# Other homes for x, the output weights and the spatial weights in a delta-rule and gated-MLP kernel on one core

## The chip, the cores and the metric

The kernel runs on one NeuronCore of a Trainium2 chip. The core has five engines with their own instruction streams: TensorE (PE) multiplies matrices from SBUF into PSUM; VectorE (DVE), ScalarE (ACT) and GpSimd (POOL) work on tensors element by element; SyncE (SP) issues all the DMAs here. They wait for each other by semaphores alone. POOL cannot reach PSUM, so whatever comes out of a matmul passes DVE or ACT.

The metric is the device time of one execution in microseconds, as the median of several runs.

## The reference

Attention by the delta rule, whose output is the input of a gated MLP. All is fp32.

```python
# q, k, v: (4, 8, 768, 48); beta: (4, 8, 768)
k_n = k / (norm(k, axis=-1) + 1e-6)
state = zeros((B, H, D, D))
for t in range(S):
    y[:, :, t] = einsum('bhd,bhde->bhe', q[:, :, t], state)
    v_old = einsum('bhde,bhd->bhe', state, k_n[:, :, t])
    state = state + beta_t * einsum('bhd,bhe->bhde', k_n[:, :, t], v[:, :, t] - v_old)
x = y.transpose(0, 2, 1, 3).reshape(4, 768, 384)

h = maximum(x @ w_in, 0.0)                  # w_in: (384, 1024)
u, v = h[..., :512], h[..., 512:]
v_n = (v - mean(v)) / sqrt(var(v) + 1e-6)   # over the last axis
v_s = einsum('ts,bsd->btd', w_spatial, v_n) + b_spatial[None, :, None]
out = (u * v_s) @ w_out                     # w_out: (512, 384)
```

## The kernel before

**The recurrence.** Time is cut into chunks of 64 tokens. Two batches with their 8 heads run side by side, so there are 24 steps: 0 to 11 for batches 0 and 1, 12 to 23 for batches 2 and 3. A step (`step`, with `kqt`) is a chain: `kqt` multiplies K and Q on PE and DVE masks the product (L801); PE multiplies K by the state, DVE subtracts that from v (L827); PE applies the chunk's solved triangle and ACT copies the result (L856); PE multiplies it by K again and DVE adds that to the state (L869, a copy at L871 in steps 0 and 12); PE makes the outputs and ACT copies them (L886).

**The groups.** Four steps make a group, and their triangular systems are solved together in advance by `prep(g)`. Its long part, the lane work, is a column by column sweep of multiplications (L647) and additions (L652). `LANES` gives it to DVE or POOL: for groups 1 and 3 all of it runs on POOL, in the tile set B; for groups 2, 4 and 5 it is shared between DVE and POOL, in the set A; group 0 is solved by blocks of 16. Behind the lane work stand a transpose on DVE and copies and memsets of halves on ACT and POOL; then `widen(g)` finishes the solve with matmuls, and the group's steps may start.

**The MLP.** Two steps make a pair J of 128 tokens in each of two batches. `convert(J)` splits the pair's x into a high and a low fp32r part (tiles xh and xl). Each product is made as high x high, high x low and low x high. `mlp_v` and `mlp_u` multiply x by `w_in` (V matmuls of 128x512, 18 a pair; U matmuls of 128x256, 36 a pair), `norm_v` and `split_v` make v_n of it. `gate(b)` follows for a batch when its six pairs are there: `mlp_g` multiplies v_n by the spatial weights (gate matmuls of 128x256, in three thirds of two halves, 36 each), DVE adds the bias (L1020), u is multiplied in, the result is split again, and `mlp_o` multiplies it by `w_out` (output matmuls of 128x384, 24 a third). A batch has 216 gate and 72 output matmuls.

**What sets the order.** No instruction is placed by hand. `Plan.add` collects operations with what they read and write, a duration, a priority `pr` and the buffers of which they take (`acq`) or free (`rel`) a unit. `Plan.run` then goes through time and gives each engine the ready operation of lowest priority number; the table TUNE adds one number to the priority of each kind of operation in each group's phase. What comes out is emitted engine by engine, and each engine executes its list strictly in order. Where an operation may run on DVE or POOL, the plan chooses. When PE would be idle for long it is given filler, a matmul on the constant tile fl whose result nobody reads.

**Buffers that the change touches.** The pool `x` has one home, (xh, xl), and a second, (la, wl), that is given to it after the last group's solve. So a pair's x is converted when the matmuls of the pair before it are done. The pool `st` has one unit, the tile g0 of 2048 columns. Through it go three loads of spatial weights (256 rows each, L423), each split into wsp_h and wsp_l; then four loads of output weights, each decoded from 64-bit floats by a series of operations on DVE, ACT and POOL (`load_f64`, L475 to L484) and split into wout_h and wout_l. Then g0 is given to the pool `g`, which has no other unit until step 23 is done; `mlp_g` needs one to start. wsp_h, wsp_l, wout_h and wout_l are in use until then: their space holds the solved triangles of groups 0 to 2, the set B, and K for the group products. So `weights2`, called after step 11, first waits for all of that as one condition (the name "early").

K and Q of a step are loaded by `load(s)` with 120 and 126 of the tile's 128 rows, and K for the group products with 121; the rest is zero from the first loads. Each head's 48 rows lie in 64, so rows 112 to 127 are all zero.

Of the kernel before, what the change touches and what calls it, by code (L numbers as in the profile page):

```python
# [1171 lines left out]
```

## Time and profile before

| | us |
|---|---|
| timed runs | 501.27, 489.70, 496.47 |
| median of them | 496.47 |
| the profiled execution, its own time | 490.77 |
| its span, from the first to the last instruction | 489.0 |
| state copies of steps 0 and 12 (L871) start at | 71.2 and 192.2 |

The page that the prediction quotes gives for each engine the time in which it is busy, then digits for forty slices of the span (9 means at least 90% busy; PEclk is the clock granted to TensorE in tenths of full speed). A view by stage gives the same for chosen stretches. A list of groups has one line per kind of instruction, with its count and duration, and a list of waits says who waited for whom. An fp32 matmul of a step, and a filler, counts as two instructions, an fp32r matmul of the MLP as one.

### The profile page before, as it was taken

The numbers are of one execution on the slowest core, as the hardware profiler recorded it, in microseconds if no ns is written. First come the engines' busy times: TensorE is split into PE (matmuls) and PEld (weight loads), VectorE is DVE, ScalarE is ACT, GpSimd is POOL, SyncE is SP. The second block draws the span as 40 slices with busy tenths as digits, with TensorE's granted clock in tenths as the row PEclk, the third lists the DMA queues.
The fourth block names the chain that finished last, engine by engine and source line by source line (L and its number), as shares of the span: only waits on it lengthen the run. The fifth ranks groups of instructions, "written<-read, shape, count | busy, mean of one in ns | idle before, by whom it ended". The sixth has DMA issues, their size and how long they took to land.

```text
span 489.0 us, 20367 instructions
## 1 busy us (share of the span) xinstructions
PE 430.8 (88%) x9094; PEld 382.3 (78%) x9094; DVE 284.0 (58%) x636; ACT 241.8 (49%) x520; POOL 157.7 (32%) x291
## 2 busy tenths in 40 slices
PE   5818688889889998789899799999999999999997
PEld 4605576678668786768678689999998999999996
DVE  4899778987888863436979532632033433452240
ACT  4686662378826387858541341727423394131111
POOL 3149899756897740133562200000000000000000
PEclk9767557998989998999979899999999999999999
DMA  8951134522325653444551002000021000001002
GB/s 268 353 155 43 45 91 111 154 60 82 87 77 143 186 158 122 137 121 132 154 152 40 34 16 95 1 34 0 17 80 35 9 2 33 1 17 50 32 11 87
DMA packets 24882, 41.92 MB, mean 86 GB/s; under 512 B 3608, under 2 KB 13976, under 8 KB 24794
## 3 DMA queue, kind: packets, MB, share of 16 engines
q1 hardware_dynamic: 24794, 40.62, 26.9%
q8 instruction: 71, 1.16, 1.0%
q14 instruction: 17, 0.14, 0.1%
HBM read 34.71 MB, written 4.72 MB: 81 GB/s over the span
## 4 chain that ended last, share of the span: by engine, by line
PE 64%; DVE 11%; ACT 9%; issue 7%; DMA 4%; POOL 3%; SPq 1%; POOLq 0%; ACTq 0%; DVEq 0%
PE ps L542 64%; DMA bn<-in_bun 2%; DMA xs<-xs 2%; ACT wsp_h L406 1%; DVE pt L801 1%; ACT wsp_l L406 1%; DVE prod L647 1%; ACT xt L406 1%; ACT gt L939 1%; DVE ps L652 1%; DMA wout_h<-in_k_t 1%; SPq L423 1%; DVE hd L616 1%; DVE ut L481 1%; POOL hd L647 1%
## 5 line engine op out<-in xcount | busy, mean ns | idle before, releaser
L542 PE MATMUL ps<-wsp_h,vf 128*128 128x256 f32 x480 | 97.0, 287 | 0.0
L542 PEld LDWEIGHTS ps<-wsp_h,vf 128*128 128x128 f32 x480 | 78.5, 191 | 0.7
L542 PE MATMUL ps<-wsp_l,vf 128*128 128x256 f32 x240 | 68.1, 284 | 0.0
L462 POOL TENSOR_TENSOR bn<-bn,nn 128x384 f32<-128x384 f32 x24 | 22.3, 931 | 119.1 <-DMA bn<-in_bun 98.3
L1020 DVE TENSOR_TENSOR gt<-ps,bbc 128x512 f32<-128x512 f32 x24 | 16.6, 691 | 56.3 <-PE ps L542 56.3
L542 PEld LDWEIGHTS ps<-wsp_l,vf 128*128 128x128 f32 x240 | 45.7, 190 | 0.0
L652 POOL TENSOR_TENSOR wsp_l<-wsp_l,wsp_h 128x60 f32<-128x60 f32 (+15 forms) x60 | 37.9, 631 | 2.2
L542 PE MATMUL ps<-wout_h,g 128*128 128x384 f32 x128 | 34.8, 340 | 1.3 <-ACT g L1025 1.2
L647 POOL TENSOR_TENSOR wsp_h<-wsp_l 128x60 f32<-128x60 f32 (+15 forms) x60 | 33.3, 555 | 2.3
L542 PE MATMUL ps<-bn 64*64 64x64 f32 x832 | 21.0, 245 | 12.9 <-DVE pt L801 7.8
L1025 ACT CAST g<-gt 128x512 fp32r<-128x512 f32 x16 | 9.9, 620 | 43.4 <-DVE gt L460 35.4
L542 PEld LDWEIGHTS ps<-bn 64*64 64x64 f32 x832 | 17.4, 154 | 17.7 <-DVE pt L801 8.7
L652 DVE TENSOR_TENSOR ps<-ps,prod 128x192 f32<-128x192 f32 (+13 forms) x90 | 29.5, 327 | 2.2
L647 DVE TENSOR_TENSOR prod<-ps,la 128x192 f32<-128x192 f32 (+13 forms) x90 | 28.7, 319 | 2.0
L856 ACT COPY w<-ps 128x384 f32<-128x384 f32 x24 | 11.5, 478 | 28.7 <-PE ps L542 24.9
L542 PEld LDWEIGHTS ps<-wout_h,g 128*128 128x128 f32 x128 | 23.3, 188 | 2.1 <-ACT g L1025 1.5
L1041 ACT COPY ob<-ps 128x384 f32<-128x384 f32 x24 | 11.5, 479 | 27.1 <-PE ps L542 26.8
L869 DVE TENSOR_TENSOR s<-s,ps 112x384 f32<-112x384 f32 x20 | 11.0, 548 | 22.0 <-PE ps L542 18.7
L542 PE MATMUL ps<-wsp_h,bn 128*128 128x256 f32 x96 | 23.3, 282 | 0.0
L929 ACT ACTIVATE vr<-ps 128x512 f32<-128x512 f32 x22 | 13.1, 596 | 18.5 <-PE ps L542 18.4
L542 PE MATMUL ps<-wout_l,g 128*128 128x384 f32 x64 | 21.9, 342 | 0.0
L1025 ACT CAST xt<-gt 128x512 fp32r<-128x512 f32 x8 | 5.0, 620 | 34.2 <-DVE gt L460 34.2
(227 smaller groups left out, 1158.4 us busy)
## 6 DMA issues: line engine op xcount, KB each, us to landing
bn<-in_bun SPq DMA_DIRECT2D x48, 192.0 KB
bn<-in_bun SPq DMA_DIRECT2D x22, 252.0 KB
bn<-in_bun SPq DMA_DIRECT2D x22, 240.0 KB
out<-ob SPq DMA_DIRECT2D x24, 192.0 KB
vf<-in_w_in SPq DMA_DIRECT2D x6, 512.0 KB
ke<-in_k_t SPq DMA_DIRECT2D x12, 242.0 KB
g<-in_w_sp SPq DMA_DIRECT2D x3, 768.0 KB
g<-in_w_out SPq DMA_DIRECT2D x4, 384.0 KB
```

The lines of the kernel that those rows point to most:

```text
L406: (nc.scalar.copy if e == "ACT" else ENG[e].tensor_copy)(out=out_, in_=in_)
L423: return P.add("SP", dur, lambda: nc.sync.dma_start(out=out_() if callable(out_) else out_, in_=in_() if callable(in_) else in_), rd, wr, ...
L462: nc.gpsimd.tensor_tensor(out=out, in0=in0, in1=in1, op=op)
L542: nc.tensor.matmul(o, l, r, start=start, stop=stop)
L647: P.add(eng, cost(n * m), lambda: ENG[eng].tensor_tensor(out=dst if fst else pt, in0=w[:, :n, j : j + 1].broadcast_to([128, n, m]), in1=la ...
L652: P.add(eng, cost(n * m), lambda: ENG[eng].tensor_tensor(out=dst, in0=dst, in1=pt, op=ALU.add), rd=[pk], wr=[key], pr=p0 + 2)
L856: P.add("ACT", 0.48, lambda: nc.scalar.copy(out=v3(w, 192), in_=v3(pc, 512)[:, :, 0:192]), rd=["pc"], wr=[("w", s % 2)], pr=pr)
L869: P.add("DVE", 0.55, lambda: nc.vector.tensor_tensor(out=sv, in0=sv, in1=pv, op=ALU.add), rd=["pc"], wr=["S"], pr=pr)
L929: P.add("ACT", 0.6, lambda: nc.scalar.activation(out=raw_(r), in_=bank(h.unit), func=AF.Relu, accum_out=st[:, j : j + 1]), rd=[("pv", i)], ...
L1020: P.add("DVE", 0.69, lambda: nc.vector.tensor_tensor(out=gt(), in0=v3(bank(h.unit), 256), in1=bbc[0][:, th * 256 : th * 256 + 256].unsquee ...
L1025: P.add("ACT", 0.6, lambda: nc.scalar.copy(out=gv(gg)[0][:, hs], in_=gt_[t.unit]), rd=[kk], wr=[("gh", b, th, half)], pr=q)
L1041: P.add("ACT", 0.48, lambda: nc.scalar.copy(out=ob_[t.unit], in_=bank(h.unit)[:, :DM]), rd=[("po", b, th, o)], wr=[("ob", b, th, o)], pr=d ...
```

## The change

1. **x.** Pairs 2 and 4 put xh and xl into a second home, the pool `x2`: the first 1536 columns of a new tile wla, which before that holds the triangles of group 0.
2. **Output weights.** They come first. g0 is used as two halves of 768 columns (pool `st` with two units), and each of four loads of 128 rows is decoded in place, with a scratch of 384 columns per half in the tile of kd, tn6 and, later, the bias. The waits are taken apart: every operation waits for what it overwrites and no more.
3. **Spatial weights.** They come second, in six loads of 128 rows through the same two halves. wsp_l is two tiles, wla (2048 columns) and wlb (2560); the triangles of groups 0, 1 and 2 lie in wla, wlb and wsp_h. g0 is given to the gate when they are split.
4. **The bias** is loaded from `weights2`, since its tile is the scratch of the decode.
5. **K and Q** are loaded with 112 rows, after step 1, and K for the group products from step 10 on.
6. TUNE has other numbers, and the plan's time for fetching instructions, FETCH, is 4.1 in place of 3.9.

```diff
-SW, SFREE, FETCH = 30.0, 0.15, 3.9
+SW, SFREE, FETCH = 30.0, 0.15, 4.1
 TUNE = [
-    -11.9, 0, 43.3, 32.1, 0, 0, 0, 0.9, -23.9, 0, -63.7, -115.6, 13.3, -38, 12.6, -55.9, 5, -10.6, -4.4, 0.1,
+    17.4, 14.9, 0, 15.3, -55.5, 43.1, 0, -2.8, -28, 13.8, -16.3, 3.8, 2.9, -11.6, 42.6, 10.5, -1.9, 6.9,
...
-    early = [tagged(t, NT * SEQ) for t in ("wsp_h", "wsp_l")] + [tagged(t, ND * DM) for t in ("wout_h", "wout_l")]
+    early = [tagged(t, n) for t, n in (("wsp_h", NT * SEQ), ("wla", 2048), ("wout_h", ND * DM), ("wout_l", ND * DM), ("wlb", NT * SEQ - 2048))]
...
-        "B": (early[1][:, 2048:3104], early[1][:, 3104:4160], early[0][:, 4096:4352], early[0][:, 4352:4544]),
+        "B": (early[0][:, 2048:3104], early[0][:, 3104:4160], early[0][:, 4160:4416], early[0][:, 4416:4608]),
...
-    xA = lambda h: h.get(lambda u: [tagged(t, NK * 256, F32R) for t in u])
+    def xA(h):
+        def make(u):
+            if u != "x2":
+                return [tagged(t, NK * 256, F32R) for t in u]
+            return [w_("wla")[:, i * NK * 256 : (i + 1) * NK * 256] for i in range(2)]
+        return h.get(make)
+    X2 = (2, 4)
+    xp_ = lambda J: "x2" if J in X2 else "x"
...
-            return early[g // 2][:, g % 2 * 2048 : g % 2 * 2048 + 2048]
+            return early[(1, 4, 0)[g]][:, 0:2048]
...
+    P.pool("x2", ["x2"])
-    P.pool("st", ["g0"])
+    P.pool("st", [0, 1])
...
     def weights2():
-        P.add("X", 0.0, None, wr=[("x", s, q) for s in range(3 * GP) for q in ("d0", "o0", "z1", "d1")] + [("la", "B"), ("w", "B"), ("prod", "B"), ("hd", "B")] + [("ke", i) for i in range(2, 8)] + ["early", "gi", "tn6"])
-        for idx in range(NT // 2):
+        xk = lambda a, b: [("x", k, q) for k in range(a, b) for q in ("d0", "o0", "z1", "d1")]
+        P.add("X", 0.0, None, wr=xk(0, GP) + [("early", 1)])
+        P.add("X", 0.0, None, wr=xk(GP, 2 * GP) + ["gi", ("early", 4)])
+        P.add("X", 0.0, None, wr=xk(2 * GP, 3 * GP) + [("la", "B"), ("w", "B"), ("prod", "B"), ("hd", "B"), ("prod2", "B"), ("early", 0)])
+        P.add("X", 0.0, None, wr=[("ke", i) for i in range(2, 8)] + [("early", 2)])
+        P.add("X", 0.0, None, rd=[("early", 1)], wr=[("xh", J) for J in X2] + [("xl", J) for J in X2] + [("early", 3)])
+        P.add("X", 0.0, None, wr=["kd", "tn6", ("early", "e")])
+        for idx in (2, 3, 4, 5, 0, 1):
...
-            ld(lambda t=t: v3(t()[:, 0:1536], SEQ), w_sp[idx * 256 : idx * 256 + 256].rearrange("(a p) n -> p a n", p=128), wr=[key], pr=due(9) + 5 * idx, acq=[("st", h)], kb=1100)
+            ld(raw, w_sp[idx * 128 : idx * 128 + 128], wr=[key], pr=due(11) + 2 * idx, acq=[("st", h)], kb=393)
+            P.add("ACT", act_t(SEQ), lambda raw=raw, idx=idx: nc.scalar.copy(out=wsp_("wsp_h", 3 * idx, 3), in_=raw()), rd=[key, ("early", 0)], wr=[(key, "h")], pr=due(12) + 0.5 * idx)
+            for i, n in ((6, 2), (8, 1)) if idx == 2 else ((3 * idx, 3),):
+                P.add("", both(256 * n), port=True, bias=BIAS, fn=lambda e, raw=raw, i=i, n=n: tt(e, wsp_("wsp_l", i, n), raw()[:, i % 3 * 256 : (i % 3 + n) * 256], wsp_("wsp_h", i, n), ALU.subtract),
+                      rd=[key, (key, "h"), ("early", 4 if i > 7 else 3 if i < 6 else 1)], wr=[(key, "l", i)], pr=due(12) + 0.5 * idx, rel=[("st", h)])
...
         for idx in range(ND):
-            load_f64(key, w_out[idx * 128 : idx * 128 + 128, :], DM, due(12) + 3 + idx, due(9) + 20 + idx,
-                     [("st", h)], lambda t=t: t()[:, 0:768], lambda t=t: t()[:, 768:1152], st)
+            ld(raw, w_out[idx * 128 : idx * 128 + 128, :].bitcast(U32).rearrange("p (n two) -> p n two", two=2), wr=[key], pr=due(8) + 3 * idx, acq=[("st", h)], kb=393)
...
-        P.add("X", 0.0, None, rd=rd, wr=["wout"], give=[("g", "g0")])
+        P.add("X", 0.0, None, rd=[(("wout", i), "l") for i in range(ND)], wr=["wout"])
+        P.add("X", 0.0, None, rd=["wsp"], wr=[(("wout", i), z) for i in range(ND) for z in ("e", "s", "m")] + [("wout", i) for i in range(ND)], give=[("g", "g0")])
+        load_bias()
...
-            n = 121 if s >= 10 else 128
+            n = 112 if s >= 10 else 128
...
-                n = {"k": 120, "q": 126}.get(q, 128) if s > 1 else 128
+                n = 112 if s > 1 and q in "kq" else 128
```

What this does to the order is seen at two places. On PE, around the end of step 17: `pt,w` is the last matmul group of a step, `w,bn` the update of its state, `s,bn` the first group of the next step, `bn 64x64` the product of K and Q one step further, `fl` filler, `vf` the normalized v of the gate. Before:

```order
L542 MATMUL ps<-pt_68,w_72 48x64 x16
L542 MATMUL ps<-w_72,bn_70 48x48 x16
L542 MATMUL ps<-s,bn_69 64x48 x16
L542 MATMUL ps<-bn_70 64x64 x16
L542 MATMUL ps<-fl 112x256
L542 MATMUL ps<-bn_69,s 48x64 x16
L542 MATMUL ps<-bn_69,xt_1034 64x48 x16
```

And now, from the middle of what stands between the update and step 18:

```order
L587 MATMUL ps<-wlb,vf_3600 128x256
L587 MATMUL ps<-wsp_h,vf_3600 128x256
L587 MATMUL ps<-s,bn_69 64x48 x16
L587 MATMUL ps<-bn_70 64x64 x16
L587 MATMUL ps<-wsp_h,vf_4009 128x256
L587 MATMUL ps<-wlb,vf_4009 128x256
```

Gate matmuls stand between the small groups of the step, where filler stood.

On POOL, at the end of the lane work of group 1 (its rows read and write wsp_h and wsp_l alone before, wsp_h alone after; those with wl, la and hd belong to group 2; `bn,nn` scales v of a step). Before:

```order
L462 TENSOR_TENSOR bn_70<-bn_70,nn 128x384
L647 TENSOR_TENSOR hd<-wl,la 128x39
L652 TENSOR_TENSOR wl<-wl,hd 128x13x3
L647 TENSOR_TENSOR hd<-wl,la 128x28
L652 TENSOR_TENSOR wl<-wl,hd 128x14x2
L647 TENSOR_TENSOR hd<-wl,la 128x15
L434 MEMSET wsp_l 128x1056
L697 MEMSET wsp_h 32x32x32 x2
```

And now (g with its number is the tile g0, `bbc` the scratch):

```order
L484 TENSOR_TENSOR g_279<-g_279,bbc 128x384
L692 TENSOR_TENSOR wsp_h<-wsp_h 128x31
L484 TENSOR_TENSOR bn_70<-bn_70,nn 128x384
L697 TENSOR_TENSOR wsp_h<-wsp_h 128x31
L484 TENSOR_TENSOR g_279<-g_279 128x384
L697 TENSOR_TENSOR wl<-wl,hd 128x14x2
L484 TENSOR_TENSOR g_279<-g_279,bbc 128x384
L692 TENSOR_TENSOR hd<-wl,la 128x15
L484 TENSOR_TENSOR wout_l<-g_279,wout_h 128x384
```

Four of the five operations of the output weights' decode that POOL does stand within nine rows of the end of group 1's lane work.

More of the change, by code (lines that the diff above doesn't have):

```diff
@@ L510, in weights2 @@
-            ld(lambda t=t: v3(t()[:, 0:1536], SEQ), w_sp[idx * 256 : idx * 256 + 256].rearrange("(a p) n -> p a n", p=128), wr=[key], pr=due(9) + 5 * idx, acq=[("st", h)], kb=1100)
-            cols = slice(idx * 1536, idx * 1536 + 1536)
-            for z in range(2):
-                cols = slice(idx * 1536 + z * SEQ, idx * 1536 + z * SEQ + SEQ)
-                k2 = (key, z)
-                P.add("X", 0.0, None, rd=[key, "early"], wr=[k2])
-                split_w(lambda t=t, z=z: t()[:, z * SEQ : z * SEQ + SEQ], k2, lambda cols=cols: w_("wsp_h")[:, cols], lambda cols=cols: w_("wsp_l")[:, cols], SEQ, due(12) + idx, [("st", h)])
@@ L517, in weights2 @@
-        P.add("X", 0.0, None, rd=[((("wsp", i), z), "l") for i in range(NT // 2) for z in range(2)], wr=["wsp"])
+            raw = lambda h=h: g0_()[:, h.unit * 768 : h.unit * 768 + 768]
+            ld(raw, w_sp[idx * 128 : idx * 128 + 128], wr=[key], pr=due(11) + 2 * idx, acq=[("st", h)], kb=393)
[3 more added lines that the diff above has]
+                      rd=[key, (key, "h"), ("early", 4 if i > 7 else 3 if i < 6 else 1)], wr=[(key, "l", i)], pr=due(12) + 0.5 * idx, rel=[("st", h)])
@@ L518, in weights2 @@
+        P.add("X", 0.0, None, rd=[(("wsp", k), "l", i) for k, i in ((0, 0), (1, 3), (2, 6), (2, 8), (3, 9), (4, 12), (5, 15))], wr=["wsp"])
+        n = DM
         for idx in range(ND):
@@ L528, in weights2 @@
-        rd = [((("wout", i), "s"), "l") for i in range(ND)]
-        P.add("X", 0.0, None, rd=rd, wr=["wout"], give=[("g", "g0")])
+            raw = lambda h=h: g0_()[:, h.unit * 768 : h.unit * 768 + 768].bitcast(U32).rearrange("p (n two) -> p n two", two=2)
+            w0, w1 = (lambda raw=raw: raw()[:, :, 0]), (lambda raw=raw: raw()[:, :, 1])
+            st = lambda w0=w0: w0().bitcast(F32)
+            e = lambda h=h: aux[:, h.unit * 384 : h.unit * 384 + 384]
+            eu = lambda e=e: e().bitcast(U32)
@@ new lines, in weights2 @@
+            d, a, pr = 0.05 + 0.68e-3 * n, 0.16 + 1.1e-3 * n, due(9) + 2 * idx
+            ek, sk = (key, "e"), (key, "s")
+            ld(raw, w_out[idx * 128 : idx * 128 + 128, :].bitcast(U32).rearrange("p (n two) -> p n two", two=2), wr=[key], pr=due(8) + 3 * idx, acq=[("st", h)], kb=393)
+            P.add("DVE", d, lambda w1=w1, eu=eu: nc.vector.tensor_scalar(
+                out=eu(), in0=w1(), scalar1=20, scalar2=0x7FF, op0=ALU.logical_shift_right, op1=ALU.bitwise_and), rd=[key, ("early", "e")], wr=[ek], pr=pr - 2, port=True)
@@ new lines, in weights2 @@
+            P.add("ACT", a, lambda eu=eu, e=e: nc.scalar.activation(out=e(), in_=eu(), func=AF.Relu, bias=cst[:, 0:1]), rd=["cst"], wr=[ek], pr=pr)
+            P.add("ACT", a, lambda e=e: nc.scalar.activation(out=e(), in_=e(), func=AF.Relu, scale=-1.0, bias=cst[:, 1:2]), rd=["cst"], wr=[ek], pr=pr)
+            P.add("ACT", a, lambda eu=eu, e=e: nc.scalar.activation(out=eu(), in_=e(), func=AF.Identity, scale=-(2.0**23), bias=cst[:, 2:3]), rd=["cst"], wr=[ek], pr=pr)
+            P.add("ACT", a, lambda w0=w0, st=st: nc.scalar.activation(out=st(), in_=w0(), func=AF.Identity, scale=2.0**-52, bias=1.0), rd=[key], wr=[sk], pr=pr)
@@ new lines, in weights2 @@
+            P.add("DVE", dve_t(n), lambda w1=w1, eu=eu: nc.vector.scalar_tensor_tensor(
+                out=eu(), in0=w1(), scalar=0x80000000, in1=eu(), op0=ALU.bitwise_and, op1=ALU.bitwise_or), rd=[key], wr=[ek], pr=pr - 2, port=True)
+            P.add("DVE", d, lambda w1=w1: nc.vector.tensor_scalar(out=w1(), in0=w1(), scalar1=0xFFFFF, scalar2=None, op0=ALU.bitwise_and), wr=[(key, "m")], rd=[key, ek], pr=pr - 2, port=True)
+            P.add("ACT", a, lambda w1=w1: nc.scalar.activation(out=w1().bitcast(F32), in_=w1(), func=AF.Copy, scale=2.0**-20), wr=[(key, "m")], pr=pr)
@@ new lines, in weights2 @@
+            P.add("", both(n), port=True, bias=BIAS, fn=lambda z, st=st, w1=w1: tt(z, st(), st(), w1().bitcast(F32), ALU.add), rd=[(key, "m")], wr=[sk], pr=pr)
+            P.add("", both(n), port=True, bias=BIAS, fn=lambda z, st=st, e=e: tt(z, st(), st(), e(), ALU.mult), rd=[ek], wr=[sk], pr=pr)
+            P.add("ACT", act_t(n), lambda st=st, cols=cols: nc.scalar.copy(out=w_("wout_h")[:, cols], in_=st()), rd=[sk, ("early", 2)], wr=[(key, "h")], pr=due(12) + idx)
+            P.add("", both(n), port=True, bias=BIAS, fn=lambda z, st=st, cols=cols: tt(z, w_("wout_l")[:, cols], st(), w_("wout_h")[:, cols], ALU.subtract),
+                  rd=[sk, (key, "h")], wr=[(key, "l")], pr=due(12) + idx, rel=[("st", h)])
@@ L707, in go @@
             return bbc[0]
-        ld(go, b_sp.unsqueeze(0).broadcast_to([128, SEQ]), wr=["kd", "tn6", "bbc"], pr=due(9), kb=384)
+        ld(go, b_sp.unsqueeze(0).broadcast_to([128, SEQ]), wr=["kd", "tn6", "bbc"] + [(("wout", i), "e") for i in range(ND)], pr=due(12), kb=384)
     def widen(g):
@@ L904, in convert @@
         ks_ = [("xk", J, hh) for hh in range(2)]
-        P.add("ACT", act_t(768), lambda: nc.scalar.copy(out=xA(x)[0], in_=xs_(xo)[:, 0:768]), rd=ks_ + [("xs", J)], wr=[("xh", J)], pr=due(2 * J + 1) + 6, acq=[("x", x)])
+        P.add("ACT", act_t(768), lambda: nc.scalar.copy(out=xA(x)[0], in_=xs_(xo)[:, 0:768]), rd=ks_ + [("xs", J)], wr=[("xh", J)] + ([("x", k, q) for k in range(GP) for q in ("d0", "o0", "z1", "d1")] if J == X2[0] else []), pr=due(2 * J + 1) + 6, acq=[(xp_(J), x)])
         P.add("", both(768), port=True, bias=BIAS if J < 7 else 0.0, fn=lambda e: tt(e, xA(x)[1], xs_(xo)[:, 0:768], xA(x)[0], ALU.subtract),
@@ L979, in mlp_u @@
         first = o == 0 and half == 0
-        chunks(mms, 3, 0.117, [("xh", J), ("xl", J), "win"] + ([] if first else [("ua", b0, th)]), [("pu", J, half)] + ([("ua", b0, th)] if first else []), pr, [("pm", h)] + ([("u", u_h[b0 + j, th]) for j in range(2)] if o == 0 and half == 0 else []), [("x", x)])
+        chunks(mms, 3, 0.117, [("xh", J), ("xl", J), "win"] + ([] if first else [("ua", b0, th)]), [("pu", J, half)] + ([("ua", b0, th)] if first else []), pr, [("pm", h)] + ([("u", u_h[b0 + j, th]) for j in range(2)] if o == 0 and half == 0 else []), [(xp_(J), x)])
         def ev(j):
```

23 lines of the change are left out of this document (12 added, 11 removed), and 45 rows, old and new, of the table TUNE.

## The prediction

> **What bounds the kernel now.** I read the page from the top: busy shares, then the forty slices, then busy time by stage, then the waits of TensorE, then the one tile (g0) through which all late weights pass.
>
> ```profile
> span 489.0 us, 20367 instructions
> PE 430.8 (88%) x9094; PEld 382.3 (78%) x9094; DVE 284.0 (58%) x636; ACT 241.8 (49%) x520; POOL 157.7 (32%) x291
> ...
> PE   5818688889889998789899799999999999999997
> ...
> PEclk9767557998989998999979899999999999999999
> ```
>
> TensorE (PE) carries the span: from slice 26 on it is full, and only the first 300 us have holes and a lowered granted clock. The same by stage (columns: stretch, its length, busy time and instructions of each engine, granted clock, DMA share, GB/s):
>
> ```profile
> 0.00:37.00 37.00, 17.79 (x350) 14.31 (x350) 28.23 (x68) 24.35 (x42) 11.85 (x23) 0.79 0.80 257
> 37.00:98.00 61.00, 48.62 (x1829) 38.87 (x1832) 51.94 (x101) 31.32 (x64) 54.00 (x105) 0.71 0.31 90
> 98.00:183.00 85.00, 77.48 (x2479) 63.87 (x2482) 69.72 (x183) 55.00 (x127) 58.94 (x112) 0.96 0.39 114
> 183.00:259.00 76.00, 66.22 (x2102) 53.85 (x2095) 44.97 (x106) 49.71 (x110) 26.98 (x47) 0.93 0.46 138
> 259.00:306.00 47.00, 41.66 (x692) 39.21 (x691) 24.86 (x56) 11.67 (x26) 5.04 (x5) 0.96 0.12 38
> 306.00:489.00 183.00, 179.01 (x1668) 172.20 (x1666) 64.28 (x127) 69.72 (x156) 0.83 (x1) 1.00 0.08 27
> ```
>
> After 306 us nothing is to be had (183.0 - 179.0 = 4.0 us, mostly the last write). From 183 to 306 us PE is idle 76.0 - 66.2 + 47.0 - 41.7 = 15.1 us. Part of its busy time there is filler, matmuls on fl that compute nothing (first line: the stage view for the tile fl alone, busy PE and PEld first), and part of the idle time ends on "issue", no wait that the profile shows, which other work fills less surely (PE's waits from 183 to 259 us: total, times, longest):
>
> ```profile
> 183.00:259.00 76.00, 6.00 (x16) 2.69 (x16) 5.32 (x8) 0.00 (x0) 0.93 0.46 138
> ...
> PE ps L542 <- issue: 6.5, 6, 1.8
> ```
>
> Why PE has nothing better to do shows the tile g0 (instruction, count, shortest/median/longest in ns, first and last start):
>
> ```profile
> L465 ACT CAST wsp_h<-g x6: 817/828/838, 172.8 to 196.3; 128x768 fp32r<-128x768 f32 x6
> L462 POOL TENSOR_TENSOR g<-g x6: 995/1011/1334, 211.9 to 254.9; 128x384 f32<-128x384 f32 x6
> L423 SPq DMA_DIRECT2D g<-in_w_out x4: 352/386/527, 199.2 to 242.3; - x4
> L475 DVE TENSOR_SCALAR g<-g x4: 349/351/406, 202.5 to 249.4; 128x384 uint32<-128x384 uint32 x4
> L477 ACT ACTIVATE g<-g,cst x4: 604/613/617, 203.4 to 249.8; 128x384 f32<-128x384 uint32 x4
> L481 DVE SCALAR_TENSOR_TENSOR g<-g x4: 546/552/560, 209.1 to 252.4; 128x384 uint32<-128x384 uint32 x4
> L465 ACT CAST wout_h<-g x4: 511/512/514, 214.0 to 256.5; 128x384 fp32r<-128x384 f32 x4
> ...
> 256.26 1.12 PE L542 MATMUL ps<-fl 128*112 128x256 f32 x4
> ...
> 258.11 0.39 PE L542 MATMUL ps<-wsp_h,vf 128*128 128x256 f32 x1
> ```
>
> One staging tile takes the spatial weights first (cast from 172.8 us, the last at 196.3), then four rounds of output weights, one load at a time (199.2 to 242.3, a round about 14 us). Only when the last round is done is g0 given to the gate, and its first matmul starts at 258.11, behind a filler. The spatial weights were there some 60 us earlier.
>
> **The change, part by part.**
>
> *Early output weights free g0 for the gate.* Counted in the order, PE has 144 gate and 24 output matmuls ahead of the last group of step 18, where before there is none, and no filler after step 4, where before eight stand in steps 18 to 20 (the 16 instructions above, each being two). The gate of batch 0 also needs all V of pairs 0 to 5, 108 matmuls: the old order has 90 by step 12 and 108 by step 15, the new one 108 by step 12. That is what the second home of x does; without it the gate could not start in step 14. The work itself is the same and is only moved; full-rate rows show its pitch:
>
> ```profile
> 409.00:434.00 25.00, 25.00 (x213) 25.00 (x212) 1.00 0.04 14
> 435.00:438.00 3.00, 3.00 (x19) 3.00 (x18) 1.00 0.00 0
> 386.00:391.00 5.00, 5.00 (x23) 4.05 (x22) 1.00 0.00 0
> ```
>
> These are a gate matmul at 25.0/213 = 0.117 us, an output matmul at about 3.0/18 = 0.17 and a V matmul at about 5.0/22 = 0.23. So 144 x 0.117 + 24 x 0.17 = 21 us of work stands ready for holes of 15.1 us and filler of 6.0. I credit: filler all of it, 6.0; idle time not on issue, 15.1 - 6.5 = 8.6, I take 7; issue, half of 6.5, 3.5, as a gate matmul lasts several times as long per instruction as those of a step; clock: 66.2 us at 0.93 and 41.7 at 0.96 lose at most 4.6 + 1.7 us to it, half is 3. Sum 19.5; the ends are 6 (filler alone) and 27.4 (everything).
>
> *The decode stands in steps 0 to 4.* The order puts the four rounds beside the lane work of group 1 on POOL (the solve of four steps' triangles) and of group 2 on DVE. Both engines are full there:
>
> ```profile
> 71.00:94.00 23.00, 19.64 (x697) 15.49 (x686) 20.64 (x50) 6.35 (x15) 21.58 (x53) 0.81 0.46 133
> ...
> L647 POOL TENSOR_TENSOR wsp_h<-wsp_l x30: 257/612/939, 35.2 to 91.7; 128x60 f32<-128x60 f32 x2, 128x87 f32<-128x87 f32 x2, 128x112 f32<-128x112 f32 x2, 128x135 f32<-128x135 f32 x2
> ```
>
> POOL has 21.6 of 23 us filled, and its lane of group 1 ends about 92 us; then group 1 is transposed and steps 4 to 7 may start. Ahead of that end or just behind it stand five decode operations on POOL, 5 x 1.01 = 5.1 us. On DVE there are eight masks at 0.35 and eleven two-operand operations at 0.55, together 8.9 us. ACT gets twenty operations of at most 0.61 and four casts at 0.51, at most 14 us; it hides them, being 6.4 us busy of 23. How far DVE work delays POOL, these rows bound:
>
> ```profile
> 69.37 0.64 POOL L647 TENSOR_TENSOR wsp_h<-wsp_l 128x252 f32<-128x252 f32 x1
> 70.09 1.76 POOL L652 TENSOR_TENSOR wsp_l<-wsp_l,wsp_h 128x252 f32<-128x252 f32 x1
> 71.93 0.65 POOL L647 TENSOR_TENSOR wsp_h<-wsp_l 128x247 f32<-128x247 f32 x1
> ...
> 70.11 1.21 DVE L627 SCALAR_TENSOR_TENSOR la<-la,hd 128x1024 f32<-128x1024 f32 x1
> ```
>
> One POOL row beside a DVE operation with two SBUF operands took 1.76 us in place of about 0.65: 1.1 of that operation's 1.2 us was lost. So group 1 slips by 5.1 us (POOL's own rows) to 5.1 + 8.9 = 14 us. I take 9, nearer to the lower end, because not every DVE row meets a POOL row that has started after it. This slip costs PE in full: at the end of step 11 the order has 78 V and 108 U matmuls behind it (before: 72 and 108), so nothing is in reserve. The six V more are 6 x 0.23 = 1.4 us gained by then; as a wait the old single home costs PE next to nothing (second row of the fence on K and Q), so no more is credited to x.
>
> The Trainium skill, SBUF — State Buffer, section "SBUF: two separate sides", says that VectorE (two SBUF inputs, or a two-port mode) and GpSimd take their shared port pair as an exclusive lock for a whole instruction. The 70.09 row agrees. By that rule every decode operation of DVE would hold POOL up, and the slip would be 14 us and not 9; this is the first rival.
>
> *Six tiles of spatial weights.* Six casts at 0.83 us as before, seven subtractions in place of six, six loads in place of three. Four of the casts now stand ahead of step 12's copy on ACT, where two stood: at most 1.7 us. The cover is PE work: 30 V and 78 U matmuls, 16 us, stand between steps 11 and 12. I take 0; without it 1.7. The bias, now loaded behind them, is wanted only by the gate's first addition in step 15: 0.
>
> *K and Q as 112 rows.* Fewer bytes per load, and PE's waits for it are small:
>
> ```profile
> PE ps L542 <- DMA bn<-in_bun: 0.6, 1, 0.6
> PE ps L542 <- ACT xh L905: 0.3, 1, 0.3
> ```
>
> The first is worth between 0 and 0.6; I take 0.5. The second is x's.
>
> **Sum.** 19.5 + 1.4 + 0.5 - 9 = 12.4 us gained. The profiled execution took 490.77 us (span 489.0), so 478.4 by its measure. It is a low one: the three timed runs are 489.70, 496.47 and 501.27, and the four times together have a mean of 494.6, 3.8 above it. A median of runs should then be 478.4 + 3.8 = 482 us, and I forecast 482.
>
> **Rivals.** *Every DVE decode row locks POOL out.* The slip is 14 in place of 9, giving 487. For it speaks the 70.09 row; against it, that the masks have one tensor operand and no row shows what they do.
>
> *The slip is hidden.* POOL idles between group 1's lane (91.7) and group 3's, which starts later:
>
> ```profile
> L647 POOL TENSOR_TENSOR wsp_h<-wsp_l x30: 252/556/652, 105.9 to 166.7; 128x60 f32<-128x60 f32 x2, 128x87 f32<-128x87 f32 x2, 128x112 f32<-128x112 f32 x2, 128x135 f32<-128x135 f32 x2
> ```
>
> If group 3's end (about 167), which holds step 12, does not move, the 9 us come back: 473. Against it: group 3 waits for group 1's tile set and not for POOL.
>
> *The gate's evictions stall PE: slower.* Each half of a gate third must be added on DVE before its bank comes free. Before, this runs after 259 us with DVE half idle (24.9 of 47); in the new order eight halves stand in steps 14 to 19, beside the lane work of group 5 on DVE. PE executes in order, so a late bank stops the step's matmuls behind it too. If each half stalls PE by d, the time is 482 + 8d: past 496.5 from d = 1.8 us, and 502 at d = 2.5, which is some four lane rows of 0.6 us in front. For it: DVE is 20.6 of 23 us busy beside a lane at 71 to 94. Against: between the halves stand small steps that leave DVE time.
>
> *The change does not do what it says.* If the six tiles, through two halves of g0, finish so late that the gate's place at step 14 arrives before them, PE waits where it has filler now; the gain falls to the clock and the six V, and with the slip of 9 the time is about 494.6 + 9 - 4.4 - 0.5 = 499.
>
> **How the numbers follow.** Forecast case 0.45 (476 to 488, its own range from credits of 14 to 25.5), lock-out 0.18 (487), hidden slip 0.17 (473, down to 465 with all 27.4 credited), stalled evictions 0.12 (490 to 508), late tiles 0.08 (499). The range 469 to 499 leaves about 2 in 10 out. A measurement of this kernel tells about 2% from no change: under 486.5 is faster, over 506.4 slower. Faster: most of the forecast case (0.34), the hidden slip (0.17) and a little of the lock-out, 0.56; slower: the far part of the stalled evictions, 0.06; the rest, 0.38, is within.
>
> **What would show it.** In the new profile, the first gate matmul before 230 us, PE idle between 183 and 306 us under 8 us in place of 15.1 and no fl row there would show the gain; POOL's lane of group 1 ending near 101 in place of 92, and group 3's near 176 in place of 167, the slip. Long waits of PE for the gate's addition in steps 14 to 19 would make the third rival right. The forecast is wrong if steps 4 to 11 slip by more than 20 us, or if PE's holes before 183 us shrink, which I credit with nothing.

## The result, and the profile after

| | before | after |
|---|---|---|
| timed runs, us | 489.70, 490.44, 496.47, 501.27 | 471.35, 471.89, 472.53, 473.46 |
| median, us | 493.46 | 472.21 |
| profiled execution, its own time and its span, us | 490.77, 489.0 | 473.46, 471.8 |

The ratio is 0.960 with a 95% interval of 0.950 to 0.969: the changed kernel is faster by 4%. The ratios here leave out runs that lie over 1.5% above the fastest of their kernel, such as the one of 501.27 us. Four runs of before are counted here, one more than the prediction had. The forecast of 482 us was 10 us too high; its range of 469 to 499 us holds the result, but the range of its forecast case, 476 to 488, does not.

The top of the page of the changed kernel, its two rows of TensorE among them, answers to the first lines quoted in the prediction:

```profile
span 471.8 us, 20342 instructions
PE 424.1 (90%) x9080; PEld 378.3 (80%) x9080; DVE 286.7 (61%) x635; ACT 239.4 (51%) x519; POOL 162.6 (34%) x294
...
PE   5827767998878999898999999999999999999997
...
PEclk9787555799978999999999999999999999999999
```

TensorE does its work in 424 us instead of 431, and is full from slice 20 on. Where the time went shows the view by stage (columns as in the prediction):

```profile
0.00:37.00 37.00, 20.39 (x382) 16.07 (x382) 29.32 (x73) 26.14 (x43) 14.41 (x27) 0.83 0.77 254
37.00:98.00 61.00, 47.96 (x1773) 39.27 (x1769) 55.94 (x127) 39.47 (x81) 53.34 (x96) 0.63 0.32 88
98.00:183.00 85.00, 76.42 (x2315) 62.63 (x2307) 71.04 (x158) 48.83 (x113) 64.25 (x121) 0.94 0.39 111
183.00:242.00 59.00, 54.16 (x1645) 46.67 (x1648) 28.74 (x65) 40.10 (x92) 10.83 (x11) 1.00 0.36 104
242.00:289.00 47.00, 46.13 (x975) 42.92 (x968) 40.23 (x95) 16.55 (x36) 17.23 (x38) 1.00 0.24 74
289.00:472.00 183.00, 178.99 (x2027) 170.73 (x2025) 61.48 (x123) 68.34 (x155) 2.49 (x3) 1.00 0.11 37
```

In the last 183 us TensorE is busy for 179.0 us in both kernels, with somewhat different work (2027 instructions here, 1668 before). Cut in this way, the 17.2 us between the two spans lie in the stage from 183 us to 183 us before the end: it lasts 106 us (289 - 183) where it lasted 123 (306 - 183). TensorE is idle there for 106 - 54.2 - 46.1 = 5.7 us instead of 15.1, it runs no filler instead of 6.0 us of it, and its granted clock is 1.00 instead of 0.93 and 0.96. Up to 183 us it is idle for 16.6 + 13.0 + 8.6 = 38.2 us; before, by the same three rows, for 19.2 + 12.4 + 7.5 = 39.1. How much work it has done by then is counted further down.

The filler and the gate's start are read from the same stage for the tile fl (busy PE and PEld first) and from the timeline of TensorE (start, duration, operation):

```profile
183.00:289.00 106.00, 0.00 (x0) 0.00 (x0) 4.80 (x8) 0.00 (x0) 1.00 0.31 91
```

```profile
217.66 0.62 PE L587 MATMUL ps<-xl,win_h 128*128 128x256 f32 x3
218.11 0.28 PE L587 MATMUL ps<-wsp_h,vf 128*128 128x256 f32 x1
```

The first gate matmul starts at 218.1 us instead of 258.1, right behind other work of the MLP. The tile view of g0 shows why (instruction, count, shortest/median/longest in ns, first and last start):

```profile
L445 SPq DMA_DIRECT2D g<-in_w_sp x6: 328/346/410, 103.9 to 206.2; - x6
L539 ACT CAST wsp_h<-g x6: 824/831/836, 187.1 to 211.0; 128x768 fp32r<-128x768 f32 x6
L445 SPq DMA_DIRECT2D g<-in_w_out x4: 327/362/382, 21.2 to 87.4; - x4
...
L569 ACT CAST wout_h<-g x4: 536/546/567, 82.8 to 104.0; 128x384 fp32r<-128x384 f32 x4
```

The output weights are done at about 105 us, and the last cast of the spatial weights starts at 211.0, later than before (196.3); but no other weights follow it in g0 any more.

The other side of the change shows in the steps. These are starts read from the timelines of both kernels (a step's state is the last write of its chain; a lane is the lane work of one group on GpSimd):

| us | before | after |
|---|---|---|
| state of step 1 | 78.9 | 83.0 |
| lane of group 1, first start to end | 34.7 to 92.4 | 32.8 to 100.7 |
| state of step 4 | 113.8 | 120.1 |
| lane of group 3, end | 167.3 | 180.1 |
| state of step 12 | 192.2 | 208.5 |
| first gate matmul | 258.1 | 218.1 |

### The profile page after: what moved, and what is told of

It is laid out like the page before. It is cut to its first block, busy times and chain, and to the rows that moved or that the text cites. A ratio compares the mean times of both kernels' runs of the same rounds, so it can differ in the third digit from the quotient of the medians.

```text
span 471.8 us, 20342 instructions
## 1 busy us (share of the span) xinstructions
PE 424.1 (90%) x9080; PEld 378.3 (80%) x9080; DVE 286.7 (61%) x635; ACT 239.4 (51%) x519; POOL 162.6 (34%) x294
## 4 chain that ended last, share of the span: by engine, by line
PE 61%; DVE 15%; ACT 12%; DMA 5%; issue 4%; POOL 3%; SPq 1%; ACTq 0%; POOLq 0%; DVEq 0%
PE ps L587 61%; DMA bn<-in_bun 3%; DVE ps L697 2%; DVE prod L692 2%; ACT gt L984 1%; ACT vr L998 1%; ACT xt L788 1%; ACT vf L1006 1%; ACT pi L784 1%; ACT xt L427 1%; DVE pt L846 1%; DMA wout_h<-in_k_t 1%; DMA xs<-xs 1%; DVE ut L503 1%; DVE wla L482 1%
## 5 line engine op out<-in xcount | busy, mean ns | idle before, releaser
L484 POOL TENSOR_TENSOR bn<-bn,nn 128x384 f32<-128x384 f32 x24 | 22.1, 920 | 95.7 <-DMA bn<-in_bun 41.2
L1065 DVE TENSOR_TENSOR gt<-ps,bbc 128x512 f32<-128x512 f32 x24 | 16.6, 690 | 53.6 <-PE ps L587 53.5
L692 POOL TENSOR_TENSOR wsp_h<-wsp_h 128x31 f32<-128x31 f32 (+15 forms) x62 | 36.8, 594 | 8.2 <-DVE wsp_h L672 6.1
L587 PE MATMUL ps<-wlb,vf 128*128 128x256 f32 x140 | 39.4, 281 | 0.0
L697 POOL TENSOR_TENSOR wsp_h<-wsp_h 128x60 f32<-128x60 f32 (+15 forms) x60 | 36.5, 609 | 1.7
L587 PE MATMUL ps<-wla,vf 128*128 128x256 f32 x100 | 28.1, 281 | 0.0
L587 PE MATMUL ps<-wout_h,g 128*128 128x384 f32 x96 | 26.4, 342 | 0.0
L587 PEld LDWEIGHTS ps<-wlb,vf 128*128 128x128 f32 x140 | 26.3, 188 | 0.0
L587 PE MATMUL ps<-wout_h,xt 128*128 128x384 f32 x96 | 25.6, 338 | 0.0
L1030 ACT ACTIVATE ut<-ps 128x256 f32<-128x256 f32 x48 | 15.6, 377 | 13.8 <-PE ps L587 13.7
L1070 ACT CAST g<-gt 128x512 fp32r<-128x512 f32 x12 | 7.4, 619 | 28.5 <-DVE gt L482 21.1
L901 ACT COPY w<-ps 128x384 f32<-128x384 f32 x24 | 11.5, 479 | 19.9 <-PE ps L587 19.7
L846 DVE TENSOR_TENSOR pt<-ps,fl 128x512 f32<-128x512 f32 x24 | 16.3, 680 | 6.7 <-PE ps L587 6.6
```

The costliest lines, as they stand in the source:

```text
L484: nc.gpsimd.tensor_tensor(out=out, in0=in0, in1=in1, op=op)
L587: nc.tensor.matmul(o, l, r, start=start, stop=stop)
L692: P.add(eng, cost(n * m), lambda: ENG[eng].tensor_tensor(out=dst if fst else pt, in0=w[:, :n, j : j + 1].broadcast_to([128, n, m]), in1=la ...
L697: P.add(eng, cost(n * m), lambda: ENG[eng].tensor_tensor(out=dst, in0=dst, in1=pt, op=ALU.add), rd=[pk], wr=[key], pr=p0 + 2)
L846: P.add("DVE", 0.69, lambda: nc.vector.tensor_tensor(out=pt.rearrange("p (d c t) -> p d c t", d=2, t=64), in0=pq.rearrange("p (d c) -> p d ...
L901: P.add("ACT", 0.48, lambda: nc.scalar.copy(out=v3(w, 192), in_=v3(pc, 512)[:, :, 0:192]), rd=["pc"], wr=[("w", s % 2)], pr=pr)
```

## The experiments

Each kernel was timed beside kernel before on the same chip; medians of the same kernel differ by a few us between chips, so ratios are given too. The changed kernel itself was not timed again beside these runs: where one of them is set against it by medians, a few us of the difference may not be the edit's. The span is that of the profiled execution. The order is planned anew wherever an edit changes what the plan sees, with the numbers of TUNE kept.

**1. The gate's tile given late.** Everything of the change stays, but g0 is given to the gate only after step 19.

```diff
-        P.add("X", 0.0, None, rd=["wsp"], wr=[(("wout", i), z) for i in range(ND) for z in ("e", "s", "m")] + [("wout", i) for i in range(ND)], give=[("g", "g0")])
+        P.add("X", 0.0, None, rd=["wsp"], wr=[(("wout", i), z) for i in range(ND) for z in ("e", "s", "m")] + [("wout", i) for i in range(ND)])
...
+        if s == 19:
+            P.add("X", 0.0, None, rd=["wsp", ("xs", 9)], give=[("g", "g0")])
```

> The changed kernel, with g0 given to the gate only when the pair of steps 18 and 19 is done, as late as before the change; all else as changed. The order stays the same to step 13; then 22 fillers stand in steps 14 to 20 where 144 gate and 24 output matmuls stood. Theory (the gain is gate work in the holes and in the place of filler between 183 and 306 us): most of the 21 us comes back, 485 to 493. Rival (the gain is the new order by TUNE, and where the gate starts matters little): 471 to 477.

Measured: 490.74 us, ratio 1.002 (0.999 to 1.005), span 489.1. The whole gain is gone. The stage from 183 to 306 us for the tile fl shows what stands in the gate's place:

```profile
183.00:306.00 123.00, 13.45 (x44) 6.69 (x44) 6.14 (x9) 0.00 (x0) 0.97 0.32 93
```

13.45 us of filler, 22 of them, and a gate that starts at 259.6 us. So the new numbers of TUNE and FETCH, the second home, the halves and the 112 rows bring nothing on balance unless the gate may start early.

**2. One home for x.** All pairs use (xh, xl) again.

```diff
-    xp_ = lambda J: "x2" if J in X2 else "x"
+    xp_ = lambda J: "x"
```

> The changed kernel, with all pairs of x in the one pool of homes as before the change; the plan is made anew. 108 V matmuls are done by step 16 in place of 12, the gate starts in step 17 in place of 14, and five fillers more are planned. Theory (the second home only brings the V of pair 5 forward so that the gate can start): a part of the gain is lost, 476 to 484. Rival (the old home never holds PE up, its wait was 0.3 us): 471 to 474.

Measured: 483.77 us, ratio 0.985 (0.976 to 0.994), span 483.3. More than half of the gain is lost with a gate that starts at 245.6 us instead of 218.1. The loss lies where the gain lay. From 183 us to 182 us before the end (301 us):

```profile
183.00:301.00 118.00, 106.64 (x2764) 93.54 (x2751) 66.38 (x153) 54.60 (x125) 22.43 (x43) 0.93 0.30 90
```

The stage is 118 us long and TensorE is idle for 11.4 us of it. Step 12's state comes at 192.6 us here, as early as before, so the 16 us by which it is late in the changed kernel are not the price of the decode, which stands at the same place here. By 195 us the changed kernel has begun 90 V and 171 U matmuls, this one 81 and 144: it goes on with the steps instead. That the pair ahead still holds the one home is the likely reason; it was not tried apart.

**3 and 4. The rows of K and Q.** The changed kernel with the old rows, and kernel before with 112 rows. The first edit is shown; the second is its reverse, made in kernel before.

```diff
-            n = 112 if s >= 10 else 128
+            n = 121 if s >= 10 else 128
...
-                n = 112 if s > 1 and q in "kq" else 128
+                n = {"k": 120, "q": 126}.get(q, 128) if s > 1 else 128
```

> The changed kernel with K and Q loaded as 120 and 126 rows and K of the groups as 121, the order unchanged. Theory (loads are hidden; PE waited 0.6 us for them in all): 472 to 473. Rival (the loads run over more queues with 112 rows and that carries part of the gain): 476 or more.

> The kernel before with 112 rows of K and Q, its order unchanged. Theory (loads are hidden): within 1 us of the kernel before. Rival (the loads carry part of the gain): 4 us or more below it, and perhaps less scatter of its runs.

Measured: old rows 474.58 us (471.82 to 474.90), ratio 0.965 (0.958 to 0.972); before with 112 rows 491.07 us (485.65 to 499.98), ratio 0.998 (0.994 to 1.003). Neither differs from its own kernel by more than the runs scatter. The rows are worth nothing that can be measured, and they are not why the changed kernel's runs lie closer together.

**5. The decode without VectorE's and GpSimd's part.** The same order; the masks, additions and multiplications of the decode are not issued. The conversions, casts and subtractions remain.

```diff
-            P.add("DVE", d, lambda w1=w1, eu=eu: nc.vector.tensor_scalar(
-                out=eu(), in0=w1(), scalar1=20, scalar2=0x7FF, op0=ALU.logical_shift_right, op1=ALU.bitwise_and), rd=[key, ("early", "e")], wr=[ek], pr=pr - 2, port=True)
+            P.add("DVE", d, lambda w1=w1, eu=eu: None, rd=[key, ("early", "e")], wr=[ek], pr=pr - 2, port=True)
...
-            P.add("DVE", dve_t(n), lambda w1=w1, eu=eu: nc.vector.scalar_tensor_tensor(
-                out=eu(), in0=w1(), scalar=0x80000000, in1=eu(), op0=ALU.bitwise_and, op1=ALU.bitwise_or), rd=[key], wr=[ek], pr=pr - 2, port=True)
-            P.add("DVE", d, lambda w1=w1: nc.vector.tensor_scalar(out=w1(), in0=w1(), scalar1=0xFFFFF, scalar2=None, op0=ALU.bitwise_and), wr=[(key, "m")], rd=[key, ek], pr=pr - 2, port=True)
+            P.add("DVE", dve_t(n), lambda w1=w1, eu=eu: None, rd=[key], wr=[ek], pr=pr - 2, port=True)
+            P.add("DVE", d, lambda w1=w1: None, wr=[(key, "m")], rd=[key, ek], pr=pr - 2, port=True)
...
-            P.add("", both(n), port=True, bias=BIAS, fn=lambda z, st=st, w1=w1: tt(z, st(), st(), w1().bitcast(F32), ALU.add), rd=[(key, "m")], wr=[sk], pr=pr)
-            P.add("", both(n), port=True, bias=BIAS, fn=lambda z, st=st, e=e: tt(z, st(), st(), e(), ALU.mult), rd=[ek], wr=[sk], pr=pr)
+            P.add("", both(n), port=True, bias=BIAS, fn=lambda z, st=st, w1=w1: None, rd=[(key, "m")], wr=[sk], pr=pr)
+            P.add("", both(n), port=True, bias=BIAS, fn=lambda z, st=st, e=e: None, rd=[ek], wr=[sk], pr=pr)
```

> The changed kernel in its own order, with the operations of the output weights' decode on DVE and POOL left out (masks, sign and exponent, addition, multiplication); the loads, ACT's part and the split stay. The weights are then wrong. It takes 7 us off DVE and 4 us off POOL in steps 0 to 4. The prediction's price (the slip of these steps costs PE in full): 7 to 9 us faster, 463 to 466. Rival (PE has holes ahead of step 12 that take the slip up): at most 3 us faster, 469 to 472.

Measured: 471.64 us (469.53 to 472.52), ratio 0.950 (0.945 to 0.956), span 470.1; the medians differ by 0.6 us and the spans by 1.7, where the prediction had priced this at some 9. The lane of group 1 ends at 98.2 us instead of 100.7. GpSimd did gain the time: its groups from 32 to 101 us, first in the changed kernel and then here (columns: count, busy us, mean ns, idle time before and what ended it).

```profile
L697 POOL TENSOR_TENSOR wsp_h<-wsp_h 128x60 f32<-128x60 f32 (+15 forms) x30 | 20.0, 665 | 0.9
...
L484 POOL TENSOR_TENSOR bn<-bn,nn 128x384 f32<-128x384 f32 x5 | 4.7, 938 | 1.5 <-PE ps L587 1.5
```

```profile
L695 POOL TENSOR_TENSOR wsp_h<-wsp_h 128x60 f32<-128x60 f32 (+15 forms) x30 | 17.8, 594 | 0.9
...
L484 POOL TENSOR_TENSOR bn<-bn,nn 128x384 f32<-128x384 f32 x5 | 4.1, 828 | 4.6 <-DMA bn<-in_bun 4.6
```

The lane's additions are shorter here (594 ns instead of 665), and the decode's own rows are gone. That the decode had made the additions longer is not shown by this: in kernel before, with no decode in this stretch, they take 670 ns. But the scalings of v (bn) stand between the lane's rows in GpSimd's list, and they now wait 4.6 us for their loads. VectorE in turn now waits for TensorE ahead of step 1:

```profile
82.20 0.56 DVE L912 TENSOR_TENSOR s<-s,ps 112x384 f32<-112x384 f32 x1 [3.98 <-PE ps L585]
```

In the changed kernel VectorE was busy at that place, most of it with the decode, and wrote this state at 82.98 us. So the decode filled time in which these engines would otherwise have waited for TensorE and for loads.

**6. More work on GpSimd.** The opposite: each of the three multiplications of the decode that GpSimd does is followed by two more, six in all, whose results are not read.

```diff
+    def twice(z, st, e, w1):
+        if z == "POOL":
+            nc.gpsimd.tensor_tensor(out=w1().bitcast(F32), in0=st(), in1=e(), op=ALU.mult)
...
-            P.add("", both(n), port=True, bias=BIAS, fn=lambda z, st=st, e=e: tt(z, st(), st(), e(), ALU.mult), rd=[ek], wr=[sk], pr=pr)
+            P.add("", both(n), port=True, bias=BIAS, fn=lambda z, st=st, e=e, w1=w1: (tt(z, st(), st(), e(), ALU.mult), twice(z, st, e, w1), twice(z, st, e, w1)), rd=[ek], wr=[sk], pr=pr)
```

> The changed kernel in its own order, with two more POOL operations of the same size behind each of the three multiplications of the decode that POOL does: six of about 1.0 us ahead of the end of group 1's lane or just behind it. Prediction's price: 5 to 6 us slower, 477 to 479. Rival (the holes take it up): at most 2 us slower, 472 to 474.

Measured: 477.46 us (476.42 to 481.58), ratio 0.964 (0.958 to 0.971), 5.3 us more than the changed kernel by the medians; the profiled execution is the slowest of the four, with a span of 479.9. Step 4's state comes at 127.4 us (7.3 later) and the gate at 226.8 (8.7 later). TensorE loses it before 183 us:

```profile
98.00:183.00 85.00, 70.41 (x2188) 57.66 (x2187) 66.88 (x156) 46.49 (x108) 64.55 (x119) 0.92 0.35 103
```

Idle time there is 14.6 us instead of 8.6. A further delay of the steps, by six rows of about 1 us, is paid almost in full: 5.3 us by the medians, 8.1 by the spans, though only 2.4 by the two ratios.

**7 and 8. Both kernels without the numbers of TUNE.** The table is emptied in kernel before and in the changed one.

```diff
-TUNE = [
-    17.4, 14.9, 0, 15.3, -55.5, 43.1, 0, -2.8, -28, 13.8, -16.3, 3.8, 2.9, -11.6, 42.6, 10.5, -1.9, 6.9,
...
-]
+TUNE = []
```

> The kernel before with every number of TUNE zero: the plan by its bare priorities. Only to be set against the next one. Both theories: slower than before, 495 to 530.

> The changed kernel with every number of TUNE zero. In its order the gate starts in step 17, with 96 gate matmuls by step 20, and eleven fillers fewer. Theory (the gain comes from freeing g0, whatever the numbers): 5 to 12 us below the run before it. Rival (the gain needs the numbers): within 3 us of it or above.

Measured: 515.54 us, ratio 1.040 (1.032 to 1.048), for kernel before, in two runs; 496.86 us, ratio 1.008 (1.002 to 1.013), for the changed one. Without any numbers the change is worth 18.7 us, about what it is worth with them (21.3 by the medians, 17.2 by the spans). So its gain does not rest on TUNE having been chosen again.

**9. Nearly no decode at all.** As run 5, and 16 operations of ScalarE are not issued either; its conversions of the low words and its casts remain.

```diff
-            P.add("ACT", a, lambda eu=eu, e=e: nc.scalar.activation(out=e(), in_=eu(), func=AF.Relu, bias=cst[:, 0:1]), rd=["cst"], wr=[ek], pr=pr)
+            P.add("ACT", a, lambda eu=eu, e=e: None, rd=["cst"], wr=[ek], pr=pr)
...
```

> The order of the changed kernel, with the whole decode of the output weights left out except ACT's conversion of the low words and the four casts: beside the rows of VectorE and GpSimd also 16 operations of ScalarE, about 0.6 us each, are gone, so the output weights are wrong. Theory A (once VectorE's and GpSimd's share is gone, what still delays steps 4 to 11 is not the decode but the new order itself: TensorE has other work in front of step 1 and step 4, and the scalings of v between GpSimd's lane rows wait for their loads): within 2 us of the run without VectorE's and GpSimd's share, 469 to 473 us, group 1's lane ending at 97 to 99 us, step 4's state at 117 to 120 us. Theory B (ScalarE's share, which the prediction costed at nothing, is what remained): 463 to 468 us, the lane ending near 94 us, step 4's state near 114 us.

Measured: 471.54 us (470.44 to 473.32), ratio 0.961 (0.952 to 0.971), span 468.7. The time is theory A's, to 0.1 us that of run 5. The steps agree with neither theory to the us: the state of step 1 comes at 77.9 us (5.1 earlier than in the changed kernel), the lane of group 1 ends at 95.7 (5.0 earlier), but the state of step 4 is only 3.2 us earlier, that of step 12 2.8, the gate 1.5. A gain on this chain fades from place to place, because something else is next each time. What GpSimd waits for from 32 to 105 us (total, times, longest):

```profile
POOL bn L484 <- PE ps L585: 3.2, 1, 3.2
POOL wlb L427 <- DVE wsp_h L659: 2.4, 1, 2.4
POOL bn L484 <- DMA bn<-in_bun: 2.0, 2, 1.7
```

**10. More work on VectorE.** The operation of the decode that reads two SBUF tensors is issued four times in a row in each round: 12 more of 0.55 us, 6.6 us in all.

```diff
-            P.add("DVE", dve_t(n), lambda w1=w1, eu=eu: nc.vector.scalar_tensor_tensor(
-                out=eu(), in0=w1(), scalar=0x80000000, in1=eu(), op0=ALU.bitwise_and, op1=ALU.bitwise_or), rd=[key], wr=[ek], pr=pr - 2, port=True)
+            P.add("DVE", dve_t(n), lambda w1=w1, eu=eu: [nc.vector.scalar_tensor_tensor(
+                out=eu(), in0=w1(), scalar=0x80000000, in1=eu(), op0=ALU.bitwise_and, op1=ALU.bitwise_or) for _ in range(4)][-1], rd=[key], wr=[ek], pr=pr - 2, port=True)
```

> The order of the changed kernel, with VectorE's operation on two SBUF tensors repeated three times more in each of the four rounds of the decode: 12 operations of 0.55 us, 6.6 us more on VectorE between about 73 and 98 us, the result unchanged. Theory A (a step that comes late by work on an engine other than TensorE costs TensorE nearly all of that, as the six operations added to GpSimd did; and GpSimd's rows beside it lose about half of VectorE's time): group 1's lane ends 3 to 5 us later than 100.7 us and the time rises by 3 to 6 us, to 475 to 478. Theory B (every such operation locks GpSimd out for its whole length): lane 6 to 7 us later, time up by 6 to 8 us, 478 to 480. Theory C (the slip is hidden on this side too): under 1.5 us more, up to 474 us.

Measured: 480.09 us (477.66 to 480.99), ratio 0.977 (0.967 to 0.987), span 477.6. The lane ends 5.9 us later (106.6), step 4's state 5.8 later (125.9), and the span is 5.8 longer: the added work is paid in full, near theory B's numbers. Its mechanism is not what the waits of GpSimd from 32 to 105 us show:

```profile
POOL g L484 <- DVE g L482: 4.7, 2, 2.7
```

In the changed kernel this wait is 0.5 us. GpSimd's part of the decode now waits for VectorE's part, and the lane stands behind it. The lane's own rows did not get longer: the additions take 647 ns on average, where they took 665 in the changed kernel:

```profile
L697 POOL TENSOR_TENSOR wsp_h<-wsp_h 128x60 f32<-128x60 f32 (+14 forms) x29 | 18.8, 647 | 0.9
```

## Why the prediction came out as it did

**The mechanism was right.** Early output weights free g0, the gate starts in the holes of steps 14 to 19, and nothing of the gain remains if it may not (run 1). All signs named for it are there: the first gate matmul at 218.1 us, before 230; idle time of 5.7 us between 183 us and the last 183, under 8; no fl row.

**The size of that gain was nearly right.** 19.5 us were credited: filler 6.0, idle time 7 + 3.5, clock 3. Found were 6.0 of filler and 15.1 - 5.7 = 9.4 of idle time. From 183 us on the changed kernel has about 4 us more work to do (worked out next) and takes 17.2 us less, so some 21 us were gained there, at an estimate. The 5.8 us of it that are neither filler nor idle time are left for the clock and all else; how much is the clock's was not taken apart.

**The step that failed is "This slip costs PE in full".** The slip came, and about in the size forecast: the lane of group 1 ends at 100.7 us for the 101 named, that of group 3 at 180.1 for 176. In this there is luck. With nearly no decode (run 9) these lanes still end at 95.7 and 176.5 us, against 92.4 and 167.3 in kernel before, so only 5.0 of the 8.3 us and 3.6 of the 12.8 are the decode's; the rest is the new order's.

TensorE paid less than half of the 9 us. Its idle time from 37 to 183 us rose from 19.9 to 21.6 us, but idle time alone does not show what was paid. The work begun by 183 us does (first before, then the changed kernel):

```profile
0.00:183.00 183.00, 143.89 (x4652) 117.04 (x4655) 149.88 (x349) 110.67 (x230) 124.80 (x238) 0.84 0.45 135
0.00:183.00 183.00, 144.78 (x4449) 117.97 (x4450) 156.30 (x355) 114.44 (x237) 132.00 (x243) 0.81 0.44 132
```

TensorE is busy for as long, at a slightly lower granted clock, and has begun 203 instructions fewer. Among them are 81 V and 128 U matmuls, against 74 and 144 before, which at the pitches of 0.23 and 0.117 is the same work within half a us, and one filler more. So 196 of the small instructions of steps and solves are missing. What one of them costs can be estimated from the last 183 us, in which both kernels keep TensorE busy for 179.0 us: the changed one has 416 of them more there, and 6 V, 18 U, 21 gate and 12 output matmuls fewer, 8.0 us at the prediction's pitches. That is 0.019 us each, 3.7 us for the 196, and with the V and U about 4 us in all. The argument looked at what stands behind the end of step 11 in the list and found no reserve. But the list of that stretch was itself written anew, and has V and U matmuls at the places where the steps now come later: by the state of step 4, which comes 6.3 us later, TensorE has begun 36 V instead of 21.

The second half of the failure is that the decode was priced as the only thing that holds the steps. Runs 5 and 9 take it away and win 1.7 and 3.1 us of span, while 0.6 and 0.7 us of the medians is within their scatter. In run 9 TensorE is 4 V, 16 U and 32 small instructions further by 183 us than in the changed kernel, 3.4 us of work, which fits the span. Runs 6 and 10 add 6 to 7 us of rows and lose 5 to 8 us by medians and spans. By these runs the chain through the lane is about level with TensorE's own list and with the loads of the steps: shortening it alone uncovers the next, lengthening it costs nearly in full. The bounds of 5.1 to 14 us were worked out for a chain that is alone; the lower end should have been 0.

**x.** The 1.4 us for six more V by step 11 was too narrow a reading. "Without it the gate could not start in step 14" was right, and a number belonged to it: 11.6 us between the medians of run 2 and of the changed kernel (with the caution that run 2 has numbers of TUNE that were not made for it). **K and Q**: 0.5 us credited, nothing measurable found (runs 3 and 4). **Six tiles**: costed at 0, and no wait of TensorE for them stands in its list from 183 to 289 us, whose longest entries are these:

```profile
PE ps L587 <- ACT xt L627: 1.5, 1, 1.5
PE ps L587 <- ACT pi L784: 1.4, 1, 1.4
PE ps L587 <- issue: 0.9, 1, 0.9
PE ps L587 <- DMA bn<-in_bun: 0.7, 1, 0.7
```

The second ends at 198.9 us, and in the 5 us before it ScalarE works almost without a break, with one cast of the spatial weights (0.83 us from 194.5) among its rows; up to that much of the wait may be theirs.

**From the profile to the median.** The sum was 478.4 us for the profiled execution, which took 473.46; the difference of 4.9 us is about the 5 us too much of the slip and the 1.7 too little of the gate's gain, less the 1.9 us of x and of K and Q, for which nothing apart was found. The other 3.8 us, by which the median was put above the profile, failed by itself. They assumed that the changed kernel's runs would scatter upwards as those of before did (489.7 to 501.3 us). They lie within 2.1 us in four runs, and the profiled one is the slowest of them.

**The rivals.** *The slip is hidden* came nearest: 473 us, with a measured 472.2. Its reason was wrong, since group 3's lane did move, by 13 us, and some 4 us were lost. That it came so near is luck: with no slip its sum is 469.4 us for the profiled execution, 4 less than measured, and the 3.8 us put on top made up for that. *Every DVE decode row locks POOL out* asked for 487 us. GpSimd's lane does not show it. Its additions take 670 ns in kernel before, where no decode stands beside them, 665 in the changed kernel and 655 in run 9 (first before, then run 9):

```profile
L652 POOL TENSOR_TENSOR wsp_l<-wsp_l,wsp_h 128x60 f32<-128x60 f32 (+15 forms) x30 | 20.1, 670 | 1.3
...
L695 POOL TENSOR_TENSOR wsp_h<-wsp_h 128x60 f32<-128x60 f32 (+15 forms) x30 | 19.7, 655 | 0.9
```

Run 10 shows no lengthening either, with 6.6 us more of such operations; why run 5 alone has 594 ns is open. *The gate's evictions stall PE*: the waits just shown have no entry for the gate's addition (gt, L1065), so no d was found. *The change does not do what it says* fell with the gate's start.

What stays open: with nearly no decode, steps 4 and 12 still come 3.1 and 13.5 us later than in kernel before (116.9 and 205.7 us). That is the order that the plan wrote for the changed kernel; which of its choices makes up how much was not taken apart. It costs TensorE little: by 183 us run 9 has begun 85 V and 144 U, 11 V more than kernel before, and 164 small instructions fewer, which nearly cancel at the prices above. By the medians, no kernel here that does the whole computation beats the changed one.

## What to carry to other kernels

When work is moved earlier onto busy engines, the delay of the chain there is not yet a cost: count all that the engine that sets the end can begin by a given time in the new order, the chain's own small instructions included, and price the delay by the work that is missing, with 0 as the lower bound. Where a planner keeps several chains level, removing work from one of them and adding work to it are not worth the same, so what an added cost loses says little about what its removal would bring. A buffer that frees an engine to start early (here g0) is worth what stands idle until then, but only together with the inputs of the work that starts, which may need a buffer of their own.
